# The first hundred microseconds of a delta-rule attention and MoE kernel, put in another order

## The chip, the core and the metric

The kernel runs on one core of a Trainium2 chip. The metric is device time in microseconds (us); for the kernel before, the median of three runs is 651.8 us (650.68 to 654.48).

## The reference, cut to what matters

Inputs are q, k, v of shape (4, 8, 768, 48) and beta of shape (4, 8, 768), then two weights, w_in (384 x 2048) and w_out (2048 x 384), all fp32.

```python
k_n = k / (np.linalg.norm(k, axis=-1, keepdims=True) + 1e-06)
for t in range(S):                                   # delta rule, one state per batch and head
    y[:, :, t] = np.einsum('bhd,bhde->bhe', q[:, :, t], state)
    v_old = np.einsum('bhde,bhd->bhe', state, kt)
    state = state + bt[:, :, :, None] * np.einsum('bhd,bhe->bhde', kt, vt - v_old)
...
h = np.maximum(x @ w_in, 0.0)                        # x is y as 3072 rows of 384
return (h * h @ w_out)
```

## The kernel before

**Units.** The 768 tokens are cut into 12 units of 64. In each unit the sequential rule becomes matrices of 64 x 64 for each of the 32 pairs of batch and head. `load` fetches the keys into a padded tile (`kpad`), and `normalize` scales them: squares on ACT, sums on DVE, a root on ACT, six short instructions and one long product on DVE. `static` transposes keys and queries on PE and multiplies them; the copies of the products are the tile `ap`. Its key part goes through DRAM (`to_blocks`, tensor `blocks`; `from_blocks`, tile `lt`) to lie one pair to a partition. `invert` solves the 32 x 32 triangles on DVE in 31 steps of two instructions, then writes the result to DRAM (`inv`) and reads it back as T in two forms (`tt` and `t1t`). `whole`, `solved` and `onward` (together `state_part`) use T on PE, make the new values, the state and the unit's output y. For units 0 and 1 one inverse serves both (`both`), and their query products are masked by POOL (AFFINE_SELECT) after ACT's copies.

**MoE.** `moe` turns the y of a unit (256 rows) into two fp32r halves, `x_h` and `x_l`, and multiplies these by the halves of the weights. It is the bulk of PE's work.

**Weights.** They come as 28 pieces, here w0 to w27: per quarter three of w_in (128 x 512) and four of w_out (128 x 384). `fetch` issues a piece's read on SP. A piece then passes four stations: `least` (ACT, scales in place), `words` (DVE, three instructions into two rooms), `high` (ACT, the upper half), `low` (PE, three products, and an ACT copy, the lower half). A piece's rooms come round again four pieces later, so `words` of a piece waits for the `low` of the fourth before it. Early pieces use the form above. The last seven go through `late` inside unit 1's stage, where DVE forms a remainder and PE has two cheap products.

**Order.** Inside `manual_schedule` the order of an engine's instructions is the order of the code; each waits for what it needs by semaphores. In the kernel before, PE, SP, DVE and ACT are in that set, and POOL is not. The beginning is written out by hand: 7 pieces before the inverse (`FIRST`), 4 around the third unit's normalization (`THIRD`), 10 between the steps of unit 0's `state_part` (`EARLY`). From unit 1 on, `weave` merges generators by places in the stage.

Of the kernel before, what the change touches and what calls it, by code (L numbers as in the profile page):

```python
# [12 lines left out]
AF = mybir.ActivationFunctionType  # L13
# [8 lines left out]
def kernel(  # L22
# [22 lines left out]
    nc = tc.nc  # L45
# [69 lines left out]
    rooms = [(spool, "a", "rest"), (mpool, "r", "h_l")]  # L115
    AHEAD = 21
    LAG = 3
# [14 lines left out]
    def split_weights():  # L132
# [39 lines left out]
        def scaled(n):  # L172

            for _ in range(n):
                if done[0] < len(raws):
                    ready.append(least(done[0]))
                    done[0] += 1

        def early(n):
# [8 lines left out]
        def settled():  # L188
            while waiting:
                low(*waiting.pop(0))  # L190

# [19 lines left out]

        ready, waiting, done = [], [], [0]
        return done, scaled, early, settled, late()

# [51 lines left out]
    def normalize(d):  # L266

        n2, s0, s1 = [apool.tile([P, H2], F32, name=f"{n}{d['u'] % 2}", bufs=1) for n in ("n2", "s0", "s1")]
        kn = d["kp"].rearrange("p c h d -> p (c h) d")[:, :, :D]
        for c in range(NC):  # L270
            h = slice(c * H, (c + 1) * H)
# [3 lines left out]
            nc.scalar.activation(out=sq, in_=kn[:, h], func=AF.Square)  # L275
            nc.vector.tensor_reduce(out=n2[:, h], in_=sq, axis=AX.X, op=ALU.add)
# [8 lines left out]
        nc.vector.tensor_scalar(out=s1, in0=s1, scalar1=0.5, scalar2=1e-6, op0=ALU.mult, op1=ALU.add)  # L285
        nc.vector.reciprocal(out=s1, in_=s1)
        yield
        nc.vector.tensor_tensor(out=kn, in0=kn, in1=s1.unsqueeze(2).broadcast_to(list(kn.shape)), op=ALU.mult)
        yield
# [8 lines left out]
    def static(d):  # L298
# [53 lines left out]
        def to_blocks():  # L352
            rows = ap.rearrange("p c h x t -> p (c h) x t")
            for n in range(4):
                t = slice(n % 2 * HB, (n % 2 + 1) * HB)
                queue = nc.scalar if u <= 1 and n % 2 else nc.sync
                queue.dma_start(out=room[n].rearrange("h s t -> s h t"), in_=rows[n * HB:(n + 1) * HB, :, 0, t])
            return room
# [8 lines left out]
        if u <= 1:  # L367
# [13 lines left out]
            for c in range(NC):  # L381
                for j, ps in enumerate(products(c, 1, 1)):
                    nc.scalar.copy(out=heads(c, j)[:, :, 1], in_=ps)
                for b in range(2):
                    half = ap[b * C:(b + 1) * C, c, :, 1]
                    nc.gpsimd.affine_select(out=half, in_=half, pattern=[[0, H], [1, C]], base=0, channel_multiplier=-1,
                                            compare_op=ALU.is_gt, fill=0.0)
                yield
            return
# [15 lines left out]
    def invert(d):  # L405
# [267 lines left out]

    FIRST, THIRD, EARLY = 7, 4, (3, 2, 3, 2)
    NS = 3 * (NW - (FIRST + THIRD + sum(EARLY))) + 2
    STEPS = 32
# [6 lines left out]
    split_early = True  # L683
    done, scaled, early, settled, splits = split_weights()
    engines = {mybir.EngineType.PE, mybir.EngineType.SP, mybir.EngineType.DVE, mybir.EngineType.Activation}
    with tc.manual_schedule(engines=engines):
        ds_.append(load(0))
        ds_.append(load(1))
        load_beta(ds_[0])
        fetch(6)  # L690
        load_beta(ds_[1])
# [3 lines left out]
        take(pair[0], 2)  # L695
        scaled(1)
        take(pair[0], 1)
        scaled(1)
        take(pair[1], 2)
        early(1)  # L700
        scaled(2)
        fetch(1)
        take(pair[1], 1)
        for d in pair:
            take(d, 1)
        fetch(2)
        for _ in range(1, FIRST):
            early(1)
            scaled(done[0] < FIRST)
        load_q(ds_[0])  # L710
        fetch(2)
        load_q(ds_[1])
        fetch(2)
        load_v(ds_[0])
        fetch(4)
        settled()
        for d in pair:
            take(d)
            scaled(2)
        ds_.append(load(2))  # L720
        scaled(6)
        take(invert(ds_[0]))
        fetch(2)
        load_q(ds_[2])
        fetch(3)
        load_v(ds_[1])
        load_beta(ds_[2])
        fetch(NW)
        third = normalize(ds_[2])
        take(third, 3)  # L730
        for _ in range(THIRD - 1):
            early(1)
            take(third, 1)
        early(1)
# [59 lines left out]
```

## Time and profile before

| | |
|---|---|
| median of three runs | 651.8 us |
| the profiled execution, its time | 654.3 us |
| its span, first to last instruction | 652.6 us |
| PE busy | 590.9 us (91%) |
| DVE busy | 409.9 us (63%) |
| ACT busy | 316.9 us (49%) |
| POOL busy | 35.3 us (5%) |
| mean granted PE clock | 0.958 |

PE, DVE, ACT and POOL are the engines for matmuls, vector work, activations and general work; SP only issues transfers here. "PEclk" is the share of full speed that the throttle granted. A name with a q, as SPq or ACTq, is an engine's time for issuing. In rows of the timeline the bracket at the end is the idle time before the instruction, and what ended it.

### The profile page before, as it was taken

The numbers are of one execution on the slowest core, as the hardware profiler recorded it, in microseconds if no ns is written. First come the engines' busy times: TensorE is split into PE (matmuls) and PEld (weight loads), VectorE is DVE, ScalarE is ACT, GpSimd is POOL, SyncE is SP. The second block draws the span as 40 slices with busy tenths as digits, with TensorE's granted clock in tenths as the row PEclk, the third lists the DMA queues.
The fourth block names the chain that finished last, engine by engine and source line by source line (L and its number), as shares of the span: only waits on it lengthen the run. The fifth ranks groups of instructions, "written<-read, shape, count | busy, mean of one in ns | idle before, by whom it ended". The sixth has DMA issues, their size and how long they took to land.

```text
span 652.6 us, 22946 instructions
## 1 busy us (share of the span) xinstructions
PE 590.9 (91%) x9906; PEld 552.6 (85%) x9906; DVE 409.9 (63%) x1122; ACT 316.9 (49%) x620; POOL 35.3 (5%) x61
## 2 busy tenths in 40 slices
PE   2740778988999999999999999999999999999997
PEld 1430447887999999999999999999999999999997
DVE  4696854577569489487497594794884874842221
ACT  3742466654444553645554545445536454444442
POOL 6021000000100100101001001001001010000000
PEclk9965598998999999999999999999999999999999
DMA  7686464501451632722623524417226135030000
GB/s 218 155 189 180 95 175 133 98 4 27 85 82 27 110 64 35 118 50 46 104 52 59 92 44 91 76 27 120 53 41 116 31 48 94 3 61 8 24 1 25
DMA packets 173724, 49.91 MB, mean 76 GB/s; under 512 B 165424, under 2 KB 168504, under 8 KB 173624
## 3 DMA queue, kind: packets, MB, share of 16 engines
q1 hardware_dynamic: 167960, 47.46, 36.9%
q10 hardware_dynamic: 5536, 0.98, 0.9%
q8 instruction: 78, 1.28, 0.9%
q14 instruction: 22, 0.18, 0.1%
q0 software_dynamic: 128, 0.01, 0.0%
HBM read 37.32 MB, written 11.01 MB: 74 GB/s over the span
## 4 chain that ended last, share of the span: by engine, by line
PE 81%; DVE 9%; ACT 4%; DMA 3%; issue 1%; SPq 1%; ACTq 0%; DVEq 0%
PE o L597 32%; PE h L610 31%; DVE tt L435 2%; DVE h_h L432 2%; PE g L510 2%; PE x L510 2%; PE x L534 2%; PE x L338 2%; PE x L550 1%; PE g L559 1%; PE g L338 1%; PE x L485 1%; PE o L163 1%; PE h L475 1%; PE h L576 1%
## 5 line engine op out<-in xcount | busy, mean ns | idle before, releaser
L597 PE MATMUL o<-w,h_h 128*128 128x384 f32 x768 | 204.1, 347 | 0.0
L589 DVE TENSOR_TENSOR h_l<-r,h_h 128x512 fp32r<-128x512 f32 x96 | 67.4, 702 | 170.1 <-PE o L597 93.0
L610 PE MATMUL h<-x_h,w 128*128 128x256 f32 x1152 | 170.2, 284 | 0.2 <-DVE x_l L580 0.2
L617 ACT ACTIVATE r<-h 128x512 f32<-128x512 f32 x96 | 57.5, 599 | 222.7 <-PE h L610 222.6
L610 PEld LDWEIGHTS h<-x_h,w 128*128 128x128 f32 x1152 | 155.5, 190 | 1.1 <-ACT x_h L579 0.3
L597 PEld LDWEIGHTS o<-w,h_h 128*128 128x128 f32 x768 | 134.2, 189 | 3.2
L597 PE MATMUL o<-w,h_l 128*128 128x384 f32 x384 | 130.0, 339 | 0.0
L610 PE MATMUL h<-x_l,w 128*128 128x256 f32 x576 | 100.5, 284 | 0.0
L434 DVE SCALAR_TENSOR_TENSOR tmp<-lt,bt,z 128x126 f32<-128x126 f32 (+22 forms) x310 | 95.6, 308 | 7.5
L435 DVE TENSOR_TENSOR z<-z,tmp 128x126 f32<-128x126 f32 (+22 forms) x310 | 79.2, 255 | 10.7
L610 PEld LDWEIGHTS h<-x_l,w 128*128 128x128 f32 x576 | 82.5, 190 | 0.0
L597 PEld LDWEIGHTS o<-w,h_l 128*128 128x128 f32 x384 | 72.3, 188 | 0.0
L618 ACT ACTIVATE r<-r 128x512 f32<-128x512 f32 x96 | 60.7, 632 | 3.0
L620 ACT CAST h_h<-r 128x512 fp32r<-128x512 f32 x96 | 59.5, 620 | 3.1
L163 PE MATMUL o<-r,plus 128*128 128x384 f32 (+1 forms) x20 | 12.3, 704 | 22.9 <-DVE r L146 19.5
L418 POOL MEMSET z<- 128x512 f32 x10 | 5.3, 532 | 453.5 <-DMA inv<-z 408.8
L163 PEld LDWEIGHTS o<-r,plus 128*128 128x128 f32 x20 | 3.7, 225 | 25.5 <-DVE r L146 19.6
L338 PE MATMUL x<-kq 48*64 48x64 f32 (+1 forms) x608 | 20.4, 255 | 3.5 <-ACT kq L325 3.5
L338 PEld LDWEIGHTS x<-kq 48*64 48x64 f32 x608 | 17.9, 152 | 5.6 <-ACT kq L325 4.3
L138 ACT ACTIVATE w<-w 128x384 f32<-128x384 f32 (+1 forms) x28 | 16.3, 613 | 6.0 <-DMA w<-in_moe_w_in_dram 2.9
L322 PE MATMUL x<-plus,kpad 64*128 64x64 f32 x104 | 7.6, 245 | 12.3 <-DMA w<-in_moe_w_in_dram 12.3
L163 PE MATMUL o<-w,minus 128*128 128x384 f32 (+1 forms) x21 | 17.4, 830 | 0.0
(121 smaller groups left out, 663.0 us busy)
## 6 DMA issues: line engine op xcount, KB each, us to landing
w<-in_moe_w_in_dram SPq DMA_DIRECT2D x12, 512.0 KB
w<-in_moe_w_out_dram SPq DMA_DIRECT2D x16, 384.0 KB
lt<-blocks SPq DMA_DIRECT2D x22, 256.0 KB
vt<-in_v_dram SPq DMA_DIRECT2D x48, 96.0 KB
out_dram<-a SPq DMA_DIRECT2D x46, 96.0 KB
kpad<-in_k_dram SPq DMA_DIRECT2D x88, 48.0 KB
qpad<-in_q_dram SPq DMA_DIRECT2D x88, 48.0 KB
tt<-inv SPq DMA_DIRECT2D x48, 64.0 KB
```

What stands on the lines that cost most here:

```text
L138: nc.scalar.activation(out=w1, in_=w1, func=AF.Prelu, scale=DOWN, alpha=SIGN)
L163: nc.tensor.matmul(ps, lhsT=m, rhs=y, start=(m is first[0][0]), stop=False)
L338: nc.tensor.matmul(ps[j][to * C:(to + 1) * C, p, (x - first) * C:(x - first + m) * C], lhsT=kq[rows, c, p, b, 0], rhs=kq[rows, c, p, b, x: ...
L434: nc.vector.scalar_tensor_tensor(out=tmp, scalar=bt[:, s:s + 1], op0=ALU.mult, op1=ALU.mult, **factors)
L435: nc.vector.tensor_tensor(out=z[:, :nj, s + 1:], in0=z[:, :nj, s + 1:], in1=tmp, op=ALU.subtract)
L510: nc.tensor.matmul(dst[j][to, c, p], lhsT=d["kq"][rows, c, p, b, x], rhs=state[rows, b, c, p], start=(c == 0 and p == 0) if x else True, s ...
L589: nc.vector.tensor_tensor(out=h_l, in0=r, in1=h_h.bitcast(F32), op=ALU.subtract)
L597: nc.tensor.matmul(o[i], lhsT=a[:, e, i * P:(i + 1) * P], rhs=halves["wo", ft][w], start=(ft == 0 and n == 0), stop=(ft == FT - 1 and n == 2))
L610: nc.tensor.matmul(hp[:, e], lhsT=halves["wi", (kt, ft // EACH)][w][:, f], rhs=x[:, kt], start=(n == 0), stop=(n == 3 * KT - 1))
L617: nc.scalar.activation(out=r, in_=hp, func=AF.Relu)
L618: nc.scalar.activation(out=r, in_=r, func=AF.Square)
L620: nc.scalar.copy(out=h_h, in_=r)
```

## The change

`normalize` issues both squares before the sums, so that they can be placed apart. `early` keeps two pieces scaled ahead of the one that DVE works on, and its stations can be called singly (`scaled`, `worded`, `highs`, `lows`). `to_blocks` of units 0 and 1 issues all its transfers on SP. In `invert`, unit 1's reading of T stands behind a yield, and the caller puts the values of unit 0, nine weight pieces and unit 2's queries ahead of it. The masks of units 0 and 1 stand behind the inverse in the code, and POOL joins the engines whose order is the code's. Eight pieces are split ahead of the inverse and 22 ahead of unit 1's stage, so 6 are left for that stage.

```diff
-    AHEAD = 21
+    AHEAD = 22
...
         def early(n):
             for _ in range(n):
-                if not ready:
-                    scaled(1)
-                waiting.append(high(*words(*ready.pop(0))))
-                if len(waiting) > LAG:
-                    low(*waiting.pop(0))
+                scaled(2 - len(ready))
+                worded(1)
+                highs(1)
+                lows(len(waiting) > LAG)
...
+        squares = []
         for c in range(NC):
...
-            nc.scalar.activation(out=sq, in_=kn[:, h], func=AF.Square)
-            nc.vector.tensor_reduce(out=n2[:, h], in_=sq, axis=AX.X, op=ALU.add)
-            yield
+            nc.scalar.activation(out=sq, in_=kn[:, c * H:(c + 1) * H], func=AF.Square)
+            squares.append(sq)
+        yield
+        for c, sq in enumerate(squares):
+            nc.vector.tensor_reduce(out=n2[:, c * H:(c + 1) * H], in_=sq, axis=AX.X, op=ALU.add)
+        yield
...
-                queue = nc.scalar if u <= 1 and n % 2 else nc.sync
-                queue.dma_start(out=room[n].rearrange("h s t -> s h t"), in_=rows[n * HB:(n + 1) * HB, :, 0, t])
+                nc.sync.dma_start(out=room[n].rearrange("h s t -> s h t"), in_=rows[n * HB:(n + 1) * HB, :, 0, t])
...
                     nc.scalar.copy(out=heads(c, j)[:, :, 1], in_=ps)
+            yield
+            for c in range(NC):
                 for b in range(2):
                     half = ap[b * C:(b + 1) * C, c, :, 1]
                     nc.gpsimd.affine_select(out=half, in_=half, pattern=[[0, H], [1, C]], base=0, channel_multiplier=-1,
                                             compare_op=ALU.is_gt, fill=0.0)
-                yield
+            yield
...
             if x:
+                yield
                 nc.gpsimd.memset(tt[:, :, :, :HB], 0.0)
...
-    FIRST, THIRD, EARLY = 7, 4, (3, 2, 3, 2)
-    NS = 3 * (NW - (FIRST + THIRD + sum(EARLY))) + 2
+    EARLY = (3, 3, 3, 2)
+    NS = 3 * (NW - AHEAD) + 2
...
-    engines = {mybir.EngineType.PE, mybir.EngineType.SP, mybir.EngineType.DVE, mybir.EngineType.Activation}
+    engines = {mybir.EngineType.PE, mybir.EngineType.SP, mybir.EngineType.DVE, mybir.EngineType.Activation,
+               mybir.EngineType.Pool}
...
-        ds_.append(load(2))
-        scaled(6)
-        take(invert(ds_[0]))
-        fetch(2)
-        load_q(ds_[2])
-        fetch(3)
-        load_v(ds_[1])
-        load_beta(ds_[2])
-        fetch(NW)
-        third = normalize(ds_[2])
-        take(third, 3)
-        for _ in range(THIRD - 1):
-            early(1)
-            take(third, 1)
+        inverse, third = invert(ds_[0]), normalize(ds_[2])
+        take(inverse, HB - 1)
+        take(third, 1)
+        scaled(3)
+        take(inverse, 1)
+        for d in pair:
+            take(d)
+        load_v(ds_[0])
+        fetch(5)
+        load_q(ds_[2])
+        fetch(NW)
+        take(inverse)
+        load_beta(ds_[2])
+        load_v(ds_[1])
+        take(third, 1)
+        worded(1)
+        take(third, 1)
+        highs(1)
+        worded(1)
+        take(third)
         early(1)
```

Three places in the engines' order show what moves. First POOL, behind the beta loads (`tt_110` is the room of the first inverse, `z` that of unit 2's); the brackets name whose semaphore an instruction waits for. Before:

```order
18 L258 DMA bt<-in_beta_dram 16x1x32 x4
19 L418 MEMSET z 128x512
20 L418 MEMSET tt_110 128x1024 [waits Pool_49]
21 L421 AFFINE_SELECT z<-z 64x512 [waits Pool_49] x2
22 L421 AFFINE_SELECT tt_110<-tt_110 128x1024 [waits Pool_49]
23 L386 AFFINE_SELECT ap<-ap 64x8x64 [waits Activation_49]
```

And after:

```order
18 L269 DMA bt<-in_beta_dram 16x1x32 x4
19 L432 MEMSET tt_110 128x1024 [waits Pool_49]
20 L435 AFFINE_SELECT tt_110<-tt_110 128x1024 [waits Pool_49]
21 L400 AFFINE_SELECT ap<-ap 64x8x64 [waits Activation_49]
22 L400 AFFINE_SELECT ap<-ap 64x8x64 [waits Pool_49]
23 L400 AFFINE_SELECT ap<-ap 64x8x64 [waits Activation_49]
24 L400 AFFINE_SELECT ap<-ap 64x8x64
25 L400 AFFINE_SELECT ap<-ap 64x8x64 [waits Activation_49]
```

The three instructions on `z` have left the front of POOL's queue (they now stand behind the clearing of unit 1's T room); the masks still follow the room of the first inverse, with waits for ACT's copies and for POOL itself alone.

Second ACT, from the first unit's products to the second's (`ap` and `kq` are the copies of products and transposes; L138, L156 and L165 are `least`, `high` and the copy of `low`). Before:

```order
16 L373 COPY ap<-h 128x4x64
17 L373 COPY ap<-x 128x4x64 x2
18 L373 COPY ap<-h 128x4x64
19 L357 DMA blocks<-ap 32x16x32 x2
20 L138 ACTIVATE w_139<-w_139 128x512
21 L325 COPY kq<-h 128x8x64
22 L325 COPY kq<-x 128x8x64
```

And after:

```order
17 L385 COPY ap<-h 128x4x64
18 L385 COPY ap<-x 128x4x64 x2
19 L385 COPY ap<-h 128x4x64
20 L138 ACTIVATE w_141<-w_141 128x512
21 L338 COPY kq<-h 128x8x64
22 L338 COPY kq<-x 128x8x64
```

ACT's two issues between the units are gone, and w2 stands there in the place of w1, which was scaled before the copies.

Third ACT around the reading of T (L457 and L472 are the issues of `t1t`). Before:

```order
65 L138 ACTIVATE w_441<-w_441 128x512
66 L457 DMA t1t<-inv 32x8x32 x4
67 L275 ACTIVATE r<-kpad_104 128x384 x2
68 L278 ACTIVATE s_738<-n_737 128x16
69 L156 CAST w_752<-r 128x512
```

And after:

```order
65 L285 ACTIVATE r<-kpad_104 128x384 x2
66 L138 ACTIVATE w_452<-w_452 128x512
67 L138 ACTIVATE w_454<-w_454 128x384
68 L138 ACTIVATE w_600<-w_600 128x384
69 L472 DMA t1t<-inv 32x8x32 x4
70 L291 ACTIVATE s_675<-n_674 128x16
71 L156 CAST w_766<-a 128x512
```

The third unit's squares and three more scalings now stand ahead of the issues that wait for the inverse in DRAM.

More of the change, by code (lines that the diff above doesn't have):

```diff
@@ L177, in scaled, with worded, highs, lows @@
                     done[0] += 1
+        def worded(n):
+            for _ in range(n):
+                formed.append(words(*ready.pop(0)))
+        def highs(n):
+            for _ in range(n):
+                waiting.append(high(*formed.pop(0)))
+        def lows(n):
+            for _ in range(n):
+                low(*waiting.pop(0))
+        def settled():
+            highs(len(formed))
+            lows(len(waiting))
         def early(n):
             for _ in range(n):
-                if not ready:
-                    scaled(1)
-                waiting.append(high(*words(*ready.pop(0))))
-                if len(waiting) > LAG:
-                    low(*waiting.pop(0))
-        def settled():
-            while waiting:
-                low(*waiting.pop(0))
+                scaled(2 - len(ready))
+                worded(1)
+                highs(1)
+                lows(len(waiting) > LAG)
         def late():
@@ L210, in late @@
             yield
-        ready, waiting, done = [], [], [0]
-        return done, scaled, early, settled, late()
+        ready, formed, waiting, done = [], [], [], [0]
+        return scaled, worded, highs, lows, early, settled, late()
     def split_bank():
@@ L269, in normalize @@
         kn = d["kp"].rearrange("p c h d -> p (c h) d")[:, :, :D]
+        squares = []
         for c in range(NC):
-            h = slice(c * H, (c + 1) * H)
             sq = (apool.tile([P, H, D], F32, name="r", bufs=2) if d["u"] in (2, 3) else
                   spool.tile([P, PC], F32, name="rest")[:, :H * D].rearrange("p (h e) -> p h e", h=H))
-            nc.scalar.activation(out=sq, in_=kn[:, h], func=AF.Square)
-            nc.vector.tensor_reduce(out=n2[:, h], in_=sq, axis=AX.X, op=ALU.add)
-            yield
+            nc.scalar.activation(out=sq, in_=kn[:, c * H:(c + 1) * H], func=AF.Square)
[4 more added lines that the diff above has]
+        yield
         nc.scalar.activation(out=s0, in_=n2, func=AF.Sqrt)
@@ L683 @@
     split_early = True
-    done, scaled, early, settled, splits = split_weights()
-    engines = {mybir.EngineType.PE, mybir.EngineType.SP, mybir.EngineType.DVE, mybir.EngineType.Activation}
+    scaled, worded, highs, lows, early, settled, splits = split_weights()
+    engines = {mybir.EngineType.PE, mybir.EngineType.SP, mybir.EngineType.DVE, mybir.EngineType.Activation,
+               mybir.EngineType.Pool}
     with tc.manual_schedule(engines=engines):
@@ L689 @@
         load_beta(ds_[0])
-        fetch(6)
+        fetch(7)
         load_beta(ds_[1])
@@ L695 @@
         take(pair[0], 2)
-        scaled(1)
+        scaled(2)
         take(pair[0], 1)
         scaled(1)
+        worded(2)
         take(pair[1], 2)
-        early(1)
-        scaled(2)
+        highs(2)
         fetch(1)
         take(pair[1], 1)
+        lows(1)
         for d in pair:
             take(d, 1)
+        scaled(2)
+        worded(2)
+        highs(1)
+        lows(1)
+        for x in range(4, 8):
+            scaled(x < 7)
+            worded(1)
+            highs(1)
+            lows(1)
         fetch(2)
-        for _ in range(1, FIRST):
-            early(1)
-            scaled(done[0] < FIRST)
         load_q(ds_[0])
+        fetch(3)
+        load_q(ds_[1])
+        fetch(3)
         fetch(2)
-        load_q(ds_[1])
-        fetch(2)
-        load_v(ds_[0])
-        fetch(4)
-        settled()
+        highs(1)
+        lows(2)
+        for d in pair:
+            take(d, 3)
+            scaled(2)
+        ds_.append(load(2))
+        fetch(1)
+        scaled(4)
+        inverse, third = invert(ds_[0]), normalize(ds_[2])
[3 more added lines that the diff above has]
+        take(inverse, 1)
         for d in pair:
             take(d)
-            scaled(2)
-        ds_.append(load(2))
-        scaled(6)
-        take(invert(ds_[0]))
-        fetch(2)
+        load_v(ds_[0])
+        fetch(5)
         load_q(ds_[2])
-        fetch(3)
+        fetch(NW)
+        take(inverse)
+        load_beta(ds_[2])
         load_v(ds_[1])
-        load_beta(ds_[2])
-        fetch(NW)
-        third = normalize(ds_[2])
-        take(third, 3)
-        for _ in range(THIRD - 1):
-            early(1)
-            take(third, 1)
+        take(third, 1)
+        worded(1)
+        take(third, 1)
+        highs(1)
+        worded(1)
+        take(third)
         early(1)
```

## The prediction

> **What bounds the kernel now.** I read the page's slices first, then a table by stretch of the beginning, the chain of waits, and the timeline of each engine up to 160 us. The slices (16.3 us each) show where TensorE (PE) is the bound:
>
> ```profile
> PE   2740778988999999999999999999999999999997
> ```
>
> From the tenth slice on PE is full, and full it stays: what happens there is PE's own work, which the change leaves alone. All that it can win lies ahead of some 155 us. Four stretches, with the columns PE, PEld, DVE, ACT, POOL busy, granted clock, DMA share and GB/s:
>
> ```profile
> 67.10:79.10 12.00, 10.27 (x77) 4.96 (x78) 10.75 (x29) 4.94 (x10) 0.00 (x0) 0.50 0.25 41
> 79.10:96.60 17.50, 14.57 (x291) 9.68 (x290) 10.17 (x23) 11.99 (x27) 0.00 (x0) 0.99 0.70 179
> 96.60:103.10 6.50, 5.30 (x20) 3.14 (x21) 0.70 (x2) 2.22 (x5) 0.00 (x0) 0.50 1.05 377
> 103.30:153.60 50.30, 42.48 (x780) 39.23 (x777) 35.59 (x92) 29.73 (x59) 0.00 (x0) 0.97 0.27 45
> ```
>
> The first three run from T's reading to unit 1's stage; none is full on any one engine, and two are at half clock. The chain of waits there goes from the inverse through DVE's words, then in a ring between ACT and DVE (scale, words, upper half; the rows of 89.42 and 90.29 below are one turn), then through PE's last lows and the transposes of y, at whose end, 103.38, ACT begins x_h:
>
> ```profile
> 62.92 2.42 DMA t1t<-inv
> 102.59 0.79 PE h L576 x11
> ```
>
> So the sum is: when does x_h come, and how long is unit 1's stage behind it.
>
> **Step 1, up to the inverse.** Rows of DVE, POOL, ACT and PE, and one of SP's waits (us, times, longest):
>
> ```profile
> 9.50 0.59 DVE L285 TENSOR_SCALAR s<-s 128x16 f32<-128x16 f32 x1
> 10.53 1.65 DVE L288 TENSOR_TENSOR kpad<-kpad,s 128x768 f32<-128x768 f32 x1 [0.15 <-DMA w<-in_moe_w_in_dram]
> 14.31 0.17 DVE L285 TENSOR_SCALAR s<-s 128x16 f32<-128x16 f32 x1
> 14.92 0.96 DVE L288 TENSOR_TENSOR kpad<-kpad,s 128x768 f32<-128x768 f32 x1
> 31.23 1.23 DVE L425 TENSOR_TENSOR lt<-lt,bt 128x1024 f32<-128x1024 f32 x1 [1.00 <-DMA lt<-blocks]
> 8.54 1.52 POOL L421 TENSOR_SCALAR_AFFINE_SELECT z<-z 64x512 f32<-64x512 f32 x2
> 10.13 1.26 POOL L421 TENSOR_SCALAR_AFFINE_SELECT tt<-tt 128x1024 f32<-128x1024 f32 x1
> 17.27 1.99 ACTq L357 DMA_DIRECT2D blocks<-ap  x2
> 19.31 0.65 ACT L138 ACTIVATE w<-w 128x512 f32<-128x512 f32 x1 [2.07 <-issue]
> 22.88 1.95 PE L163 MATMUL o<-a,plus 128*128 128x512 f32 x2
> SPq L357 <- DMA w<-in_moe_w_out_dram: 1.6, 1, 1.6
> ```
>
> Beside POOL's selections unit 0's two DVE instructions take 0.59 and 1.65, unit 1's alike ones 0.17 and 0.96: 1.11 us more, and the 0.59 ends as POOL's second selection does (10.09, 10.06). With `z` gone from there POOL is done at about 9.3 in place of 11.4, but the room's own selection now falls earlier, on 8.0 to 9.3, and will hold DVE's first short ones instead. I take -0.6 (between 0 and -1.1).
>
> In the Trainium skill, "SBUF — State Buffer", section "Who interferes with whom", VectorE and GpSimd hold a shared port pair for a whole instruction and the other waits it out. Those end times agree; by this rule `z`'s selections, which now run near 65 us, could cost DVE's short chain there up to 1.5 us, which would not change the sum, since that chain has over 3 us to spare (it is wanted when step 4's second low ends).
>
> ACT's issues hold it from 17.27 to 19.31 while unit 1's transposes wait to be copied; that 2.0 goes. But DVE now has eight pieces to form before the inverse in place of seven, and w3's scaling stands on ACT behind the copy of the first low. That low, at 22.88 now, starts about 20.8, takes some 2.4 and its copy 0.6; with the scaling DVE has w3 at 24.3. Five pieces follow, four of 384 columns at 1.4 (89.42 to 90.85 in step 4's rows) and one of 512 at 1.7 (79.72 to 81.41): 31.3 without a gap between them to spare or to add, less the 0.6. SP's four issues of a unit's blocks wait in turn for w3 to w6 to land (1.6 for two of them before); unit 1's blocks decide, with products 2 us sooner and w7 ahead of them, so I let `lt` land about 30, in place of 30.6. Inverse start 30.7 against 31.23: **-0.5** (bounds +0.9, if the pieces come with gaps as before, and -2.6, both gains in full).
>
> **Step 2, the inverse.** The masks run inside it and slow it:
>
> ```profile
> 40.14 0.41 DVE L432 TENSOR_TENSOR h_h<-lt,tt 128x240 f32<-128x240 f32 x1
> 40.58 0.73 DVE L435 TENSOR_TENSOR tt<-tt,h_h 128x240 f32<-128x240 f32 x1
> 40.39 3.01 POOL L386 TENSOR_SCALAR_AFFINE_SELECT ap<-ap 64x512 f32<-64x512 f32 x4 [29.00 <-ACT ap L383]
> ```
>
> Eight instructions are longer by about 0.32, 2.6 us in all. The order shows, though, that the masks still wait for ACT's copies alone; nothing holds POOL until the inverse ends. I cost this edit at **0** (bounds 0 and -2.6).
>
> **Step 3, T's reading.** Rows of DVE, ACT and SP:
>
> ```profile
> 65.77 1.01 DVE L276 TENSOR_REDUCE n<-r 128x8 f32<-128x384 f32 x2 [6.00 <-ACT r L275]
> 65.21 0.94 ACT L275 ACTIVATE r<-kpad 128x384 f32<-128x384 f32 x2 [8.49 <-DMA t1t<-inv]
> 62.92 4.39 SPq L452 DMA_DIRECT2D tt<-inv  x8
> 75.12 1.78 SPq L457 DMA_DIRECT2D t1t<-inv  x4
> 74.66 0.43 DVE L468 STREAM_TRANSPOSE t<-t1t 128x256 f32<-128x256 f32 x1
> ```
>
> DVE is idle for 6.0 us because the squares stand behind ACT's issues of t1t. With the squares ahead, DVE does the sums (1.0) and the words of w8 and w9 (1.7 each) in that gap; what is late next is the root, behind the issues, at about 65.1. DVE then forms w10 and transposes t1t by about 69 in place of 74.66. SP stood from 67.3 to 75.12 for that transposition; now unit 0's values, nine pieces and unit 2's queries go ahead of that wait. The values are wanted at about 78 by step 4's count, the pieces from 82 on; at the 377 GB/s of the third stretch the pieces' 3.8 MB take 10 us from 68, so none is late. Unit 1's T moves behind them, to about 80, and is wanted at 128.
>
> **Step 4, from T to x_h.** Now PE carries it:
>
> ```profile
> 71.24 2.08 PE L163 MATMUL o<-a,plus 128*128 128x512 f32 x2
> 73.54 0.63 PE L164 MATMUL o<-rest,plus 128*128 128x512 f32 x1
> 79.72 0.43 DVE L146 TENSOR_SCALAR a<-w 128x512 int32<-128x512 int32 x1 [0.36 <-PE o L163]
> 80.72 0.69 DVE L150 SCALAR_TENSOR_TENSOR rest<-w 128x512 fp32r<-128x512 uint32 x1
> 83.91 0.91 PE L163 MATMUL o<-r,plus 128*128 128x384 f32 x2
> 85.01 1.02 PE L163 MATMUL o<-a,plus 128*128 128x512 f32 x2
> 86.33 1.02 PE L163 MATMUL o<-r,plus 128*128 128x512 f32 x2
> 89.42 0.36 DVE L146 TENSOR_SCALAR a<-w 128x384 int32<-128x384 int32 x1 [1.52 <-ACT w L138]
> 90.29 0.56 DVE L150 SCALAR_TENSOR_TENSOR rest<-w 128x384 fp32r<-128x384 uint32 x1
> 98.39 1.65 PE L163 MATMUL o<-r,plus 128*128 128x384 f32 x2 [1.20 <-ACT w L165]
> 100.47 1.48 PE L163 MATMUL o<-a,plus 128*128 128x384 f32 x2
> L559 PE MATMUL g<-vt,ap 64*64 64x48 f32 x64 | 1.1, 218 | 0.0
> ```
>
> A low of 384 columns takes 1.10 at full clock (83.91 to 85.01) and 2.08 at half (98.39 to 100.47); one of 512 takes 1.32 and 2.93 (71.24 to 74.17). Before, the last four pieces came a ring apart (DVE idle 1.52 for ACT's scaling, some 2.9 us a piece), PE cooled down over it, and its last lows ran at half clock. With two pieces scaled ahead the ring is open and PE sets the pace. SP's issues of T's first half end about 65.1; with some 2.4 to land (as t1t in the chain) and the 0.5 of step 1 T is there at 67.0. Then 64 products of L475 and two lows of 512 at half clock, 1.1 + 5.9: 74.0. I let the clock be full from there: in the rows above it came after 12 us with a gap of 1.6, and after 6.5 without a long one; this stretch has none, so I take 7. Then L485 0.7; twelve lows, eight of 384 and four of 512, 8.8 + 5.3; three rounds of 64 state products at 1.1; the transposes of y 0.8: 18.9, ending at 92.9. Waits for the two PSUM banks, whose copies stand in ACT's row behind upper halves, I put at 1.5 (as 1.20 in the row of 98.39): x_h at 94.4 against 103.38, **-9.0**. Bounds: -10.5 without waits; with half clock to the end the lows take 28.4 in place of 14.1, the other products 8.0 in place of 4.0, and x_h comes at about 111.
>
> The Trainium skill, "TensorE: Matmul & The Clock Gate", Part 1 (The HAM clock gate), releases the clock after one busy window of about 3.4 us. No stretch here needed so little from its first product, so the trace disagrees; by the rule the second low would already be quick, and the sum 1.6 us better, inside the range.
>
> **Step 5, unit 1's stage.** Its waits on PE, with us, times and longest:
>
> ```profile
> PE x L163 <- DVE w L170: 4.5, 4, 3.1
> PE x L163 <- DVE ap L348: 1.8, 1, 1.8
> ```
>
> One piece fewer is split there: two PE products, an estimated 0.7 (half a low's 1.32), and some 2 us of DVE (words, and a remainder like them). w22 comes scaled: ACT has two scalings ahead of the first upper half in place of three, and the masks of unit 2 come about 1.3 sooner, off the 1.8. The 3.1 is the last remainder, behind DVE's row of words, inverse steps and remainders; in the second half of the stage there are two pieces to form in place of three, some 1.9 less. That is up to 3.9; as PE may find another wait behind each, I take **-3.0** (bounds 0 and -3.9). Later stages: 0.
>
> **Sum.** Step 1's -0.5 is in step 4's start; -9.0 - 3.0 = -12.0. The profiled execution took 654.3, so 642.3; it stood 2.5 above the median, and against 651.8 I get **640 us**. The runs spread by 0.6%, so about 0.5% (3.3 us) is what can be told from no change.
>
> **Rivals.**
> - *Half the gain.* PE is warm only from about 79, as before (2.6 more), and ACT's row, which serves four stations and the unit's chain in strict order, delays a few lows by 0.5 each (2 to 3); 6.5 us are won, 645.3. For it speaks that only one of the two cold stretches ended sooner.
> - *Given back.* x_h comes early, but unit 1's stage waits for what it waited for before and step 5's 3.1 grows; 9 to 12 are lost again: 649 to 652. For it: DVE has 35.6 of 50.3 us to do there. Against it: that part shrinks by a piece.
> - *Masks truly behind the inverse.* -2.6 more: 637.5. Against it stands their place in POOL's row.
> - *The change doesn't do what it says* in its other parts (the ring stays, since the words still wait for the low of the fourth piece before): as half the gain, and counted there.
> - *Slower.* TensorE stays at half clock to the end of the beginning: by step 4's bound x_h at 111, 7.6 later than now, less step 5's 3.0: about 656.4. It decides once more than some 12 of the 18 us of warm work run cold. For it: 96.6 to 103.1 at 0.50; against it: 79.1 to 96.6 at 0.99 with gaps larger than the new ones.
>
> **How the numbers follow.** Chances: forecast 0.61, half 0.22, given back 0.08, masks held 0.05, slower 0.04. The range 635 to 647 takes in the forecast, the masks and most of the half gain, and leaves out given back and slower: about 0.85 inside, less what a run's own spread takes. Faster by over 0.5% is below 648.5: 0.61 + 0.22 + 0.05 and a little of given back, 0.89; within 0.5%: 0.07; slower: 0.04.
>
> **What would show it.** DVE's first inverse step near 31.8; masks still at 40 to 51 with 0.73 beside them; DVE's sums right behind the inverse, at about 59; SP's issues unbroken from 63 to 80; L138 no longer the releaser of L146 after 85; clock full from about 74 without a second fall before unit 1's stage; x_h near 94. Wrong it is if the last lows still run at 0.50, if SP's blocks stand long for w6, or if the stage behind x_h grows.

## The result, and the profile after

| | before | after |
|---|---|---|
| median of the runs shown (4 each) | 652.7 us (650.68 to 654.48) | 637.01 us (636.73 to 637.46) |
| ratio, 95% interval | | 0.9761 [0.9729, 0.9793] |
| profiled execution, its span | 654.32, 652.6 | 636.73, 635.0 |
| mean granted clock | 0.958 | 0.969 |
| x_h (ACT's first copy of unit 0's y) | 103.37 | 93.70 |
| unit 1's stage, from x_h to the next x_h | 56.55 | 48.05 |
| from there to the span's end | 492.7 | 493.2 |

The span is 17.6 shorter: 9.7 of it lie ahead of x_h, 8.5 in unit 1's stage, and 0.5 come back later. The page's slices of PE and of its clock, 15.9 us each:

```profile
PE   2950799889999999999999999999999999999997
...
PEclk9965699999999999999999999999999999999999
```

PE is full from the tenth slice on, nearly so from the sixth, and the clock, once up in the fifth, stays up. By stretch (columns as in the prediction: length, busy time and count of PE, PEld, DVE, ACT, POOL, granted clock, DMA share, GB/s); the second fence has the same stage in the kernel before:

```profile
66.96:70.38 3.42, 3.12 (x65) 2.02 (x66) 3.10 (x7) 0.88 (x2) 0.00 (x0) 0.50 0.82 153
70.38:73.79 3.41, 3.41 (x14) 1.53 (x17) 2.48 (x6) 1.51 (x4) 0.00 (x0) 0.50 1.03 366
73.79:93.70 19.91, 19.16 (x324) 12.62 (x325) 12.49 (x27) 15.54 (x34) 0.00 (x0) 1.00 0.68 170
93.70:141.75 48.05, 44.12 (x824) 41.85 (x822) 36.62 (x96) 29.59 (x61) 0.00 (x0) 1.00 0.35 60
```

```profile
103.37:159.92 56.55, 48.73 (x825) 45.23 (x822) 38.50 (x100) 32.06 (x63) 0.00 (x0) 0.94 0.24 40
```

From 73.79 to x_h PE is idle for 0.75 of 19.9 us, all at full clock. In unit 1's stage its idle time went from 7.82 to 3.93 and its busy time from 48.73 to 44.12, although the split of one piece is all that left the stage. The timelines after, behind the inverse and at the start, one fence each for DVE, SP and POOL:

```profile
8.30 1.07 DVE L293 TENSOR_SCALAR s<-s 128x16 f32<-128x16 f32 x1 [0.28 <-ACT s L291]
...
10.72 0.96 DVE L301 TENSOR_TENSOR kpad<-kpad,s 128x768 f32<-128x768 f32 x1 [0.15 <-DMA w<-in_moe_w_in_dram]
...
24.07 0.36 DVE L146 TENSOR_SCALAR r<-w 128x384 int32<-128x384 int32 x1 [4.11 <-ACT w L138]
...
30.96 1.22 DVE L439 TENSOR_TENSOR lt<-lt,bt 128x1024 f32<-128x1024 f32 x1
...
59.46 1.00 DVE L289 TENSOR_REDUCE n<-r 128x8 f32<-128x384 f32 x2
...
62.97 0.69 DVE L150 SCALAR_TENSOR_TENSOR h_l<-w 128x512 fp32r<-128x512 uint32 x1
64.96 0.52 DVE L293 TENSOR_SCALAR s<-s 128x16 f32<-128x16 f32 x1 [1.30 <-ACT s L291]
...
69.30 0.44 DVE L483 STREAM_TRANSPOSE t<-t1t 128x256 f32<-128x256 f32 x1
```

```profile
65.24 2.72 SPq L242 DMA_DIRECT2D vt<-in_v_dram  x4
...
70.72 7.60 SPq L248 DMA_DIRECT2D qpad<-in_q_dram  x8
...
80.64 2.56 SPq L467 DMA_DIRECT2D tt<-inv  x4
```

```profile
8.07 1.26 POOL L435 TENSOR_SCALAR_AFFINE_SELECT tt<-tt 128x1024 f32<-128x1024 f32 x1
39.91 3.23 POOL L400 TENSOR_SCALAR_AFFINE_SELECT ap<-ap 64x512 f32<-64x512 f32 x4 [30.57 <-ACT ap L395]
47.42 2.98 POOL L400 TENSOR_SCALAR_AFFINE_SELECT ap<-ap 64x512 f32<-64x512 f32 x4 [4.29 <-ACT ap L395]
```

The gap of 6.0 behind the inverse is filled: sums at 59.46, words of w8 and w9 until 63.66, 1.30 idle for the root. The masks (the last two rows) still run inside the inverse, which goes from 30.96 to 59.55. SP stood for 7.7 us before the reading of t1t; now its longest wait between 62.7 and 80.6 is 1.2. What PE still waits for in unit 1's stage (us in total, times, longest):

```profile
PE x L163 <- DVE w L170: 2.1, 1, 2.1
PE x L163 <- DVE vt L533: 1.6, 1, 1.6
```

### The profile page after: what moved, and what is told of

Same layout as the page of the kernel before. It is cut to its first block, busy times and chain, and to the rows that moved or that the text cites. A ratio compares the mean times of both kernels' runs of the same rounds, so it can differ in the third digit from the quotient of the medians.

```text
span 635.0 us, 22958 instructions
## 1 busy us (share of the span) xinstructions
PE 585.2 (92%) x9908; PEld 548.3 (86%) x9908; DVE 409.9 (65%) x1121; ACT 316.2 (50%) x620; POOL 35.6 (6%) x61
## 4 chain that ended last, share of the span: by engine, by line
PE 86%; DVE 8%; DMA 2%; ACT 1%; issue 1%; SPq 1%; DVEq 0%
PE o L612 33%; PE h L625 32%; PE o L163 2%; PE x L351 2%; DVE h_h L446 2%; DVE tt L449 2%; PE g L525 2%; PE x L525 2%; PE x L549 2%; PE x L565 2%; PE g L574 2%; PE g L351 2%; PE h L490 1%; PE x L500 1%; PE h L591 1%
## 5 line engine op out<-in xcount | busy, mean ns | idle before, releaser
L490 PEld LDWEIGHTS h<-tt,ap 32*32 32x32 f32 x768 | 8.2, 109 | 22.5 <-ACT w L156 19.2
L490 PE MATMUL h<-tt,ap 32*32 32x32 f32 x768 | 9.6, 198 | 19.4 <-DMA tt<-inv 19.4
L291 ACT ACTIVATE s<-n 128x16 f32<-128x16 f32 x12 | 2.6, 216 | 39.9 <-DVE n L289 31.8
L506 ACT ACTIVATE tt<-x 32x256 f32<-32x256 f32 x44 | 16.4, 373 | 0.6
```

The costliest lines, as they stand in the source:

```text
L490: nc.tensor.matmul(ps[at[h % 2][b], h // 2], lhsT=ap[lower[b], c, e, 0, :HB], rhs=tt[lower[b], c, e, HB:], start=True, stop=True)
L506: nc.scalar.mul(out=right[upper[b], j, :, HB:], in_=ps[j][upper[b]], mul=-1.0)
```

## The experiments

The open question was unit 1's stage: 8.5 us where the sum had 3.0. The theory: 3.9 of it are waits, about 1.2 the piece, and the rest two falls of the clock that the kernel before had and this one has not. The rivals: the piece alone does it; or the open ring and SP's order do. The same runs tell what carries x_h. All medians below stand against medians of 651.9 to 652.3 for the kernel before on the same chip (the changed kernel's against 652.7), and the ratios, taken over the executions, need not equal those of the medians; "masks held" means that POOL's masks are kept back until the inverse ends, "late steps" are the steps of `late`; "cold" is the number of stretches of 3.41 us at clock 0.50 within the stage of the profiled run.

| kernel | x_h | stage | PE idle in it | cold | median us (range) | ratio to before |
|---|---|---|---|---|---|---|
| before | 103.37 | 56.55 | 7.82 | 2 | 652.2 | |
| ring alone | 96.30 | 57.48 | 8.79 | 2 | 646.66 (642.97 to 647.91) | 0.9886 [0.9847, 0.9926] |
| ring and T's order | 98.06 | 54.41 | 6.08 | 2 | 644.21 (643.63 to 646.6) | 0.9884 [0.9859, 0.9909] |
| changed, 21 pieces | 91.30 | 52.80 | 5.86 | 1 | 640.08 (638.73 to 640.13) | 0.9799 [0.9775, 0.9824] |
| changed, ring kept | 94.10 | 50.78 | 4.84 | 1 | 640.02 (637.61 to 640.28) | 0.9795 [0.9767, 0.9824] |
| changed, squares late | 96.39 | 48.06 | 3.93 | 0 | 639.97 (639.35 to 641.06) | 0.9814 [0.9792, 0.9836] |
| changed, sums thrice | 92.82 | 52.69 | 5.97 | 2 | 640.23 (639.49 to 640.83) | 0.9824 [0.9808, 0.984] |
| **changed** | 93.70 | 48.05 | 3.93 | 0 | 637.01 (636.73 to 637.46) | 0.9761 [0.9729, 0.9793] |
| T together (masks held) | 92.27 | 47.78 | 3.93 | 0 | 635.81 (635.26 to 636.52) | 0.9752 [0.9729, 0.9775] |
| masks held | 91.20 | 49.27 | 3.91 | 1 | 635.76 (635.13 to 636.54) | 0.9739 [0.9715, 0.9763] |
| held, 0.84 | 91.24 | 49.75 | 3.10 | 2 | 635.29 (633.39 to 635.75) | 0.9736 [0.9715, 0.9756] |
| held, 0.84, sums later | 91.18 | 47.64 | 2.18 | 1 | 634.12 (633.67 to 634.43) | 0.9724 [0.9709, 0.9738] |
| that with 23 pieces | 93.08 | 47.05 | 1.73 | 1 | 635.29 (633.89 to 636.35) | 0.9741 [0.9718, 0.9763] |
| masks held, 23 pieces | 93.11 | 45.36 | 1.75 | 0 | 633.85 (633.51 to 634.58) | 0.9718 [0.9701, 0.9735] |

**The ring alone, on the kernel before** (all calls of `early` behind the inverse pass 2; those ahead of it keep 1):

```diff
-        def early(n):
+        def early(n, ahead=1):
...
-                if not ready:
-                    scaled(1)
+                scaled(ahead - len(ready))
...
-            early(1)
+            early(1, 2)
```

> The kernel before with one edit: behind the inverse ACT scales two pieces ahead in place of one; squares, T's fetch, masks, order of the pieces and their number (21) stay as before. Theory (the open ring and the warm clock carry most of x_h's 9.7 us): the four pieces of the ring (2.9 us each) run at PE's pace, the fall of the clock to 0.50 from 96.3 to 103.1 does not come (2.7 us), x_h comes at 97 to 99 in place of 103.4; w21 comes scaled into unit 1's stage, so its stall of 1.75 behind the masks shrinks too; in all 6 to 9 us less than before, 643 to 647. Rival (the squares and T's order carry it; DVE, behind the late squares, is the pace and not ACT's scaling): x_h stays at 102 or later, at most 2 us less. Rival (x_h comes sooner, but unit 1's stage gives it back): x_h near 98, time within 2 us of before.

x_h came 7.1 sooner, a little better than expected. The clock, up at 73.05, fell once more from 76.46 to 79.87, but from there to x_h it stayed up. But the stage gave time back: its wait in front of unit 2's masks grew from 1.75 to 3.5. That wait, and a part of the chain of waits:

```profile
PE x L163 <- DVE ap L347: 3.5, 1, 3.5
```

```profile
94.13 0.58 SPq L125
...
94.75 7.80 DMA w<-in_moe_w_in_dram
...
102.57 0.02 ACT w L138
```

ACT's scaling, due early in the stage, waits for a piece that SP issued only at 94.13. So the expectation held for x_h and failed for the stall, which it had shrinking: the ring hid a late queue.

**The ring and T's order, on the kernel before** (the edit of the ring above, and these):

```diff
             if x:
+                yield
                 nc.gpsimd.memset(tt[:, :, :, :HB], 0.0)
...
-        take(invert(ds_[0]))
-        fetch(2)
+        inverse = invert(ds_[0])
+        take(inverse, HB)
+        fetch(5)
         load_q(ds_[2])
-        fetch(3)
-        load_v(ds_[1])
-        load_beta(ds_[2])
         fetch(NW)
+        take(inverse)
+        load_beta(ds_[2])
+        load_v(ds_[1])
```

> The kernel before with two edits: two pieces scaled ahead behind the inverse, and unit 1's T fetched behind the pieces and unit 2's queries, as the changed kernel does. Squares, masks and the number of pieces (21) stay as before. With the first edit alone x_h came at 96.3, but unit 1's stage took 57.5 and held a stall of 3.5: ACT's scaling waited till 102.55 for a piece that SP had issued at 94.13. Theory (SP, which stood from 67.3 to 74.7 for the transposition of t1t, made that piece late): the pieces are issued some 10 us sooner, the stall falls under 0.7 and no fall of the clock follows it, x_h 95.5 to 96.5, the stage 52 to 54.5: 640.5 to 643.5. Rival (the piece was late for the DMA's throughput, whatever SP's order): the stall stays over 2.5, 645 to 648.

```profile
PE x L163 <- DVE w L170: 4.6, 4, 3.1
...
PE x L163 <- DVE ap L347: 0.5, 1, 0.5
```

The stall is 0.5 and the stage 54.41, so SP's stand had made the piece late. The time, 644.2, is just over the range given: x_h came at 98.06, since the clock rose only at 82.13 in that execution (for good at 79.9 with the ring alone), and the 3.1 wait near the stage's end was still followed by two cold stretches.

**The ring kept, on the changed kernel**:

```diff
-                scaled(2 - len(ready))
+                scaled(1 - len(ready))
                 worded(1)
```

> The changed kernel with one edit: behind the inverse ACT scales one piece at a time, as before. Nineteen pieces are scaled by then, so the ring has the last three (w19 to w21). Theory: each costs 2.9 in place of 1.1 to 1.3, so x_h comes about 5 us later than 93.7; the gaps let the clock fall in front of x_h or not (2.6 more if so); w22 comes unscaled into unit 1's stage, 1 to 2 more there: 642 to 646. Rival (the squares and T's order carry the gain and the ring is hidden behind PE): within 1 us of the changed kernel, 636 to 638.

x_h at 94.10, 0.4 later, where the theory had 5. DVE waits for a scaling once, 1.07 us at 86.75, and PE hardly notices: its waits for a bank from 74 to 95 are 1.4 in place of 0.7. So the rival is right for x_h; and as the inverse ended at 60.02 there, 0.5 later than in the changed kernel, the ring may be worth nothing. A likely reason, not tried by itself: with the squares ahead, DVE has w8 and w9 formed before T lands, and these two pieces in hand cover the three turns that are left of the ring. The time fits neither account (636 to 638 or 642 to 646): it moves between 637.6 and 640.3 with a median of 640.0, and the profiled run, of 640.22, has a cold stretch in the stage that the changed kernel has not.

**21 pieces ahead of the stage, on the changed kernel**:

```diff
-    AHEAD = 22
+    AHEAD = 21
...
-    EARLY = (3, 3, 3, 2)
+    EARLY = (3, 3, 2, 2)
```

> The changed kernel with 21 pieces split ahead of unit 1's stage in place of 22; all else stays. Theory (of unit 1's stage's 8.5 us the piece is worth about 1.0 of PE products and up to 1.9 of waits, the rest is two falls of the clock that no longer come, 3.5, and stalls gone through scaling ahead): x_h 1.3 to 2.0 sooner than 93.7, the stage 1.0 to 3.5 longer than 47.5: the whole between 0.5 less and 2 more than the changed kernel, 636.5 to 639. Rival (the piece is the stage's gain): the stage 5 us or more longer, 640 or more.

```profile
91.30:144.10 52.80, 46.94 (x826) 43.58 (x823) 38.40 (x100) 31.44 (x62) 0.00 (x0) 0.97 0.32 56
```

```profile
PE x L163 <- DVE w L170: 5.0, 4, 3.1
```

x_h came 2.4 sooner (1.3 to 2.0 were expected; the clock rose 1.2 sooner in that execution, which an estimate, half of it, puts at 0.6) and the stage was 4.75 longer: 1.93 of idle time (5.86 to 3.93), the rest PE's busy time, 46.94 to 44.12, of which a cold stretch of 3.41 is 1.7 and the piece 1.1. The median lies 3.1 over the changed kernel, where the rival had it: the piece is worth more than the sum had, through the wait and the fall that it takes along. It isn't all: 56.55 against 52.80 at the same number of pieces is 3.75 that the rest of the change wins in the stage.

**Squares late, on the changed kernel**:

```diff
         take(inverse, HB - 1)
-        take(third, 1)
         scaled(3)
         take(inverse, 1)
+        take(third, 1)
```

> The changed kernel with the squares of the third keys back behind ACT's issues of t1t. Theory (PE sets the pace from T on; DVE's gap of 6 us comes back, but its words of w8 and w9 are then only 1 to 2 us late for their lows): first sums at about 65.5 in place of 59.5, low of w8 0.5 to 1.5 later than 68.26, x_h 0.5 to 2 later: 637.5 to 639.5. Rival (the squares carry x_h's gain): x_h 4 or more later, 641 or more. Rival (they cost nothing): within 0.3 of the changed kernel.

```profile
65.40 1.01 DVE L289 TENSOR_REDUCE n<-r 128x8 f32<-128x384 f32 x2 [5.71 <-ACT r L285]
```

```profile
76.00 0.91 PE L163 MATMUL o<-a,plus 128*128 128x384 f32 x2 [1.20 <-ACT w L165]
```

x_h 2.7 later, the stage alike, the time 3.0 more: a little over the theory's range, and short of the rival's 4. The two cold lows are not held up; the next ones are, twice by 1.2, since w10 and what follows are formed behind the root.

**Masks held behind the inverse**, on the changed kernel, by a selection on two columns of the inverse's last product:

```diff
             tmp = room[:, :nj * nt].rearrange("p (j t) -> p j t", t=nt)
+            d["last"] = room[:, :2]
...
         take(inverse, 1)
+        held = ds_[0]["last"]
+        nc.gpsimd.affine_select(out=held, in_=held, pattern=[[0, 2]], base=1, channel_multiplier=0,
+                                compare_op=ALU.is_gt, fill=0.0)
         for d in pair:
             take(d)
```

> The changed kernel, where one more selection on two columns of the inverse's last product (it changes no value) stands ahead of the masks in POOL's row and holds them until the inverse's steps end. Theory (eight inverse instructions are longer by 0.32 for the masks): the inverse ends at 57.0 in place of 59.55, T lands 2.6 sooner, and as PE carries the stretch behind it x_h comes 2 to 2.6 sooner than 93.7: 634.4 to 635. Rival (DVE pays the same behind the inverse: sums, words of w8 and w9 wait for POOL's selections, 3 us in all, and T's second half or the second low waits for them): 0 to 1 us less, 636 to 637. Rival (the masks did not slow the inverse, the lengths are the tile's): inverse end 59.5, no change.

```profile
55.85 1.24 POOL L753 TENSOR_SCALAR_AFFINE_SELECT h_h<-h_h 128x2 f32<-128x2 f32 x1 [46.52 <-DVE tt L450]
57.05 6.65 POOL L400 TENSOR_SCALAR_AFFINE_SELECT ap<-ap 64x512 f32<-64x512 f32 x8
```

```profile
55.82 1.23 DVE L452 TENSOR_TENSOR tt<-tt,bt 128x1024 f32<-128x1024 f32 x1
```

The inverse ends 2.5 sooner and x_h comes 2.5 sooner, as the theory had it. Only 1.25 reach the median, 0.8 over the theory's 635: the profiled run has one cold stretch in the stage (1.7), at a wait of 2.1 that the changed kernel has too.

**T together, on the changed kernel**:

```diff
             if x:
-                yield
                 nc.gpsimd.memset(tt[:, :, :, :HB], 0.0)
```

> The changed kernel with one edit undone: unit 1's T is fetched right behind unit 0's, so SP stands till the transposition of t1t (69.3) and all pieces, values and queries behind it are issued some 8 us later. Theory (open queue and open ring are worth their gain only together): x_h up to 1.5 later than 93.7 or the same, ACT's scaling for unit 1's stage waits for its piece, stall in front of the masks of unit 2 1 to 3.5, a fall of the clock behind it where it is over 1.75: 639 to 643. Rival (with 22 pieces split the late pieces are wanted later, the queue has slack): within 0.7 of the changed kernel.

```profile
61.22 0.52 POOL L462 MEMSET tt<- 128x512 f32 x1 [51.89 <-DVE h_l L150]
61.70 6.33 POOL L400 TENSOR_SCALAR_AFFINE_SELECT ap<-ap 64x512 f32<-64x512 f32 x8
```

It was faster than the changed kernel, which nobody had: the edit moved the clearing of unit 1's T ahead of the masks in POOL's row, and so held them behind the inverse as well (its end: 57.1). Against the kernel with masks held, x_h comes 1.1 later (92.27 to 91.20), and the stage is the same but for a cold stretch. The 1.1 need not be the fetch's alone, since the masks start 4.6 us later here (61.70 and 57.05). The stall of 3.5 that the ring alone had is not there: with 22 pieces split and the squares ahead the queue has slack.

**Late steps over 0.84 of the stage, masks held**, the first edit, **and unit 3's sums later as well**, both:

```diff
-                parts.append((splits, steps(NS, 0, 0.88)))
+                parts.append((splits, steps(NS, 0, 0.84)))
```

```diff
-            parts += [(getting, L1 + steps(6, *N1)),
+            parts += [(getting, L1 + steps(6, *((0.385, 0.785) if u == 1 else N1))),
```

> The kernel with the masks held behind the inverse, and the late pieces' steps spread over 0.84 of unit 1's stage in place of 0.88, so that the last remainder stands earlier in DVE's row. Theory (DVE's row of inverse steps, sums and h_l makes PE wait 2.1 for that remainder, and where that wait lies in one window of 3.41 us the clock falls for the next one, 1.7 more): wait under 1.0, no fall of the clock in the stage, stage 46 to 48 in place of 49.3: 633 to 635 against 635.8. Rival (DVE's row is full there, and what is moved back, h_l or the inverse steps, makes PE wait as long): within 0.5 of 635.8.

> The kernel with the masks held and the late steps spread over 0.84, and with unit 3's key sums and what follows them (unit 1's stage alone) moved 0.025 of the stage later, so that DVE subtracts from unit 1's values ahead of the sums. Theory (PE's wait of 2.7 is DVE's sums of 1.0, the transposition and the subtraction in a row; the clock falls because that wait lies in one window): wait 1.2 to 1.8, no window of 3.41 us idle for 1.75 or more, no fall; stage 45 to 46.5 against 49.75: 631 to 633 against 635.3. Rival (the wait ends with the transposition of t1t or h_l, which PE's own products release, whatever stands between): wait over 2.3, 634.5 to 636.

```profile
109.09:112.50 3.41, 1.45 (x22) 1.08 (x13) 1.85 (x4) 0.07 (x1) 0.00 (x0) 1.00 0.56 85
112.50:115.92 3.42, 2.72 (x12) 2.75 (x13) 3.09 (x11) 1.00 (x3) 0.00 (x0) 0.50 0.33 59
```

```profile
108.84:112.25 3.41, 1.67 (x35) 1.32 (x27) 1.66 (x4) 1.06 (x3) 0.00 (x0) 1.00 0.63 91
112.25:115.67 3.42, 3.42 (x15) 3.42 (x16) 3.25 (x12) 0.89 (x2) 0.00 (x0) 0.50 0.42 72
```

With 0.84 the 2.1 went (0.2 left), but the 1.6 on unit 1's values grew to 2.7 and drew two cold stretches behind it. The 635.3 lies 0.3 over the theory's range and at the edge of the rival's. With the sums behind the subtraction that wait is 1.7, as expected, yet the clock still fell once, and 634.1 is over the 631 to 633 given.

**23 pieces, masks held; and 23 pieces with the last two edits as well**:

```diff
-    AHEAD = 22
+    AHEAD = 23
...
-    EARLY = (3, 3, 3, 2)
+    EARLY = (3, 3, 3, 3)
```

> The kernel with the masks held, with 23 pieces split ahead of unit 1's stage in place of 22. Theory (from 21 to 22 the piece cost x_h 2.4 and saved the stage 1.2 of PE's work, 1.9 of waits and a fall of the clock): x_h 92.5 to 93.6 against 91.2, the stage's work at full clock 1.2 less, waits under 3 in place of 3.9, no window idle for 1.75 and so no fall: stage 45 to 46.5 against 49.3, 633 to 635.5 against 635.8. Rival (the waits that are left come from unit 3's keys and DVE's inverse steps, not from the pieces): waits stay near 3.9, the piece costs at x_h what it saves, 635 to 637.

> The kernel with the sums moved (masks held, late steps over 0.84), and 23 pieces split ahead of unit 1's stage. Theory: x_h 1.3 to 2.4 later than 91.2, the stage's work 1.2 less, its waits under 1.5, no fall of the clock: 630.5 to 633. Rival (with 22 the stage has no waits left that a piece could save): as the kernel with 22 plus 0 to 1.2, 632 to 634.

```profile
93.11:138.47 45.36, 43.61 (x821) 41.29 (x818) 34.16 (x92) 28.14 (x57) 0.00 (x0) 1.00 0.37 64
```

```profile
109.17:112.58 3.41, 2.50 (x130) 2.02 (x129) 0.00 (x0) 2.51 (x6) 0.00 (x0) 1.00 0.70 94
112.58:116.00 3.42, 3.41 (x13) 3.41 (x14) 1.33 (x3) 0.00 (x0) 0.00 (x0) 0.50 0.30 55
```

With the masks held and 23 pieces, x_h costs 1.9 and the stage saves 3.9 (2.2 of idle time, and the cold stretch of the other): 633.85, the best of all, 3.2 under the changed kernel with ranges that don't touch. With the two edits on top, the idle time is the same and a cold stretch comes in: 635.3, outside both accounts.

**Sums thrice, on the changed kernel**, which makes one wait longer:

```diff
-        for c, sq in enumerate(squares):
+        for c, sq in list(enumerate(squares)) * (3 if d["u"] == 3 else 1):
             nc.vector.tensor_reduce(...)
```

> The changed kernel where DVE does unit 3's key sums three times over (same result), 2.0 us more ahead of its subtraction from unit 1's values, on which PE waits 1.6 in unit 1's stage. Theory (a window of the clock's grid that is idle for about half of its 3.41 us drops the clock for the next one, which costs 1.7 beside the wait): PE's wait is 3.6, so that one window is idle by at least 1.8 wherever the grid falls; the clock falls behind it, unit 1's stage is 3.7 longer than 48.05 from x_h to x_h, 51.5 to 52: 640.3 to 641.1 against 637.0. Rival (a wait costs its own length, and the falls in the kernel before were a mark of something else): no fall, stage 50.0, 639.0. Rival (DVE's later idle time takes the work up and PE waits less behind it): stage under 49.5, 638.5 or less.

```profile
112.70:116.11 3.41, 0.48 (x5) 0.28 (x3) 3.41 (x9) 0.00 (x0) 0.00 (x0) 1.00 0.46 73
116.11:119.53 3.42, 2.91 (x12) 2.94 (x13) 3.18 (x12) 1.01 (x3) 0.00 (x0) 0.50 0.20 35
```

```profile
PE x L163 <- DVE vt L533: 3.4, 1, 3.4
```

The wait is 3.4, the clock falls behind it, and the median rises by 3.2 where the idle time rose by 2.0. In the profiled run a second cold stretch followed the wait near 136, in exchange for an x_h 0.9 sooner. The median lies 0.07 under the theory's range, and all five executions lie over the rival's 639.0, so this wait costs more than its length. By how much the time alone can't say, as the second stretch and the sooner x_h blur it; that the clock falls right behind the longer wait is what the rows show.

## Why the prediction was right, step by step

637.0 lies in the range, 3.0 under the 640, and the sign and the mechanism ahead of x_h were as described. In the profiled executions the sum had 642.3 and 636.7 came: 5.6 off, nearly all of it in one step. That the median is off by only 3.0 is partly luck: 2.5 were taken off the sum because the profiled execution of the kernel before stood that far above its median, while that of the changed kernel stands 0.3 under its own.

*Step 1* (-0.5): -0.27. The half that failed is POOL's front: -0.6 was taken, but the room's selection held DVE's first short instruction until it ended (8.30 + 1.07 = 9.37 against 8.07 + 1.26 = 9.33), so 0.59 + 1.65 became 1.07 + 0.96, 0.2 less. The words add up to 31.6 by the step's own prices (24.3 and 7.3), not 31.3; they began at 24.07 and took 6.9 without a gap, to 30.96. The rule cited there, from the Trainium skill's "SBUF — State Buffer", "Who interferes with whom", agrees again: with masks held, POOL's selection of two columns took 1.24 and ended with DVE's 1.23 product that ran beside it (57.09, 57.05). The 1.5 that the step put at stake near 65 came to 0.6: two of DVE's short instructions took 0.52 and 0.45 in place of 0.17 each, with no effect on the sum.

*Step 2* (0, lower bound -2.6): the masks stayed inside the inverse; the run that held them got 2.5 of the 2.6.

*Step 3*: sums 59.46 (59 given), the next thing late the root, 64.96 (65.1), t1t transposed 69.30 (69), unit 1's T 80.64 (80), nothing waited for it.

*Step 4* (x_h at 94.4): 93.70. Clock full from 73.79 (74.0 taken), waits for the banks 0.7 (1.5 taken). The words of the step, "with two pieces scaled ahead the ring is open", name the wrong part of the change for it: on the changed kernel the ring is worth at most 0.4 of x_h, the squares 2.7, T's order up to 1.1 (that with the masks held). On the kernel before, the ring alone is worth 7.1. That they cover the same gap, so that their worths don't add, fits these runs; none takes two of them out of the changed kernel at once. An x_h moves by chance too: with the sums thrice, where nothing ahead of it was edited, it came 0.9 sooner, as the clock rose at 71.74 and not at 73.79 (half of the 2.05 between is 1.0). The rival of half the gain fell with the clock's one clean rise.

*Step 5* (-3.0, bound -3.9) is the term that was mis-sized: -8.5. Its waits were taken at less than they gave: idle time went from 7.82 to 3.93, which is the step's bound by itself, without the piece. The piece's products were 1.2 (48.73 less 3.4 for two cold stretches, against 44.12) in place of 0.7. The remaining 3.4 was in no term and no rival: the kernel before ran at 0.50 twice in unit 1's stage,

```profile
109.92:113.33 3.41, 1.66 (x12) 1.37 (x11) 3.34 (x7) 2.27 (x5) 0.00 (x0) 1.00 0.00 0
113.33:116.75 3.42, 3.42 (x18) 3.42 (x17) 3.28 (x7) 2.37 (x4) 0.00 (x0) 0.50 0.48 73
150.88:154.29 3.41, 1.30 (x10) 1.30 (x11) 3.20 (x11) 0.48 (x1) 0.00 (x0) 1.00 0.35 60
154.29:157.71 3.42, 3.42 (x17) 3.42 (x16) 1.85 (x6) 0.85 (x2) 0.00 (x0) 0.50 0.00 0
```

each time behind one of the two waits that the step counted, 1.75 and 3.06. It could have been seen: the stage's clock of 0.97 (up to 153.6) and these stretches stand in the trace of before, and each of those waits cost its length and 1.7 more. "As PE may find another wait behind each" came true in part: the wait of 1.6 on unit 1's values is new. It is outweighed, since the 4.5 and 1.8 that the step listed fell to 2.1 and nothing, and a gap of the kernel before that the step did not list ("issue": no releaser is seen) is gone as well:

```profile
PE g L510 <- issue: 1.2, 1, 1.2
```

What the piece and the rest of the change each hold of this is settled only roughly: 21 pieces leave 1.9 more idle time and one cold stretch.

*The clock rule.* The prediction said of the Trainium skill's "TensorE: Matmul & The Clock Gate", Part 1 (The HAM clock gate), that the trace disagrees, since no stretch rose after one busy window. That reading was wrong for the changed kernel. By that part of the Trainium skill the window of 3413 ns is free-running, and laid on such a grid the rise of 73.79 comes right behind the first window that is busy throughout (70.38 to 73.79; the one before is idle for 0.3). The 7 us taken were a window and what was missing of the one before.

## What to carry to other kernels

Before pricing a wait of TensorE near a stretch of low clock, lay the clock's windows over it: here a wait that emptied half a window mostly cost its length and half of the next window. Edits that cover the same gap have to be tried alone and together: scaling ahead was worth 7.1 us of x_h without the other edits, and at most 0.4 beside them. And look what an edit does to the row of an engine that it isn't about: the clearing of a tile moved in POOL's row was worth 2.5 us of the inverse.

## What the runs showed of the hardware

All changes of the granted clock in unit 1's stage and ahead of it lie on a grid: in the kernel before at 79.20, 96.26, 103.09, 113.33, 116.74, 154.29 and 157.70, multiples of 3.413 us apart, and likewise in the other traces, with another offset in each (the changed kernel rose at 73.79, the kernel with masks held at 68.65). This is the free-running window that the Trainium skill's "TensorE: Matmul & The Clock Gate", Part 1 (The HAM clock gate), describes. From 58 to 628 us, the fourteen traces have 2,253 such windows at full clock. Fifteen were followed by a fall: fourteen of the fifteen in which PE was idle for 1.74 us or more, and one in which it was idle for 0.91 (the row of 109.17 above), with 2.3 us of small products (32x32 and 48x64 tiles) in the rest. One with 1.87 idle was not followed by a fall.

So in these traces about half an idle window was enough, and no wholly idle one was needed; the Trainium skill's table there speaks of an idle window of about 3.4 us, and the measurement decides. Whether the small products count for less was not tried by itself, and the rises don't settle it: of 28 half-clock windows busy for 3.38 us or more two were not followed by a rise (68.96 in the kernel before, 68.48 with the ring and T's order), both with 1.0 us of such products, but three others with as much were. A window need not be busy throughout either: with the sums thrice the clock rose behind one busy for 2.91 (the row of 116.11).

This makes a time depend on where the grid falls. The changed kernel's waits of 1.60 and 2.08 each lay across an edge,

```profile
111.34:114.75 3.41, 2.72 (x43) 2.46 (x35) 1.64 (x4) 0.26 (x2) 0.00 (x0) 1.00 0.70 97
114.75:118.16 3.41, 2.50 (x17) 2.40 (x17) 3.17 (x12) 1.79 (x5) 0.00 (x0) 1.00 0.37 65
131.82:135.23 3.41, 2.46 (x24) 2.08 (x15) 3.20 (x11) 0.94 (x3) 0.00 (x0) 1.00 0.36 62
135.23:138.64 3.41, 2.28 (x18) 2.31 (x19) 3.19 (x9) 0.48 (x1) 0.00 (x0) 1.00 0.32 60
```

and drew no fall. With the masks held, nearly all of the same wait of 2.1 lay in one window and did (first row); with the squares late it lay much the same and did not (second row), so half a window is an edge and not a sharp one:

```profile
130.09:133.50 3.41, 1.45 (x9) 1.12 (x7) 3.31 (x10) 0.06 (x1) 0.00 (x0) 1.00 0.35 59
135.44:138.85 3.41, 1.54 (x9) 1.21 (x7) 3.31 (x10) 0.16 (x1) 0.00 (x0) 1.00 0.40 69
```

Where two executions of a kernel differ by some 1.7 us or a multiple, this is a likely cause, not a shown one. The mean clocks on record fit it (with the ring kept, 0.972 for the execution of 637.61 and 0.966 for the three of 639.83 to 640.28), but where the clock fell is known for the profiled ones alone.
